# Attention of six batches in blocks of two head pairs, spread over the tiles of an MLP

## The chip, the cores and the metric

The kernel runs on one core of one Trainium2 chip. The metric is the time of one execution in microseconds (us), taken on the device. The core has TensorE (PE in the profile; its weight loads are listed apart as PEld), VectorE (DVE), ScalarE (ACT), GpSimd (POOL) and SyncE (SP), which here only issues DMA transfers.

## What is computed

The reference is a decayed causal attention followed by a mixture of four experts:

```python
# q, k, v: (8 batches, 8 heads, 576 positions, 64)
scores = scale * np.matmul(q, k.transpose(0, 1, 3, 2))
Dmat = np.where(rel >= 0, gamma ** rel, 0.0)        # gamma of the head, rel = i - j
attn = np.matmul(scores * Dmat, v)
x = attn.transpose(0, 2, 1, 3).reshape(8 * 576, 512)
p = domain_probs / domain_probs.sum(-1, keepdims=True)
for e in range(4):                                  # w1: 512 x 1024, w2: 1024 x 512
    out += p[:, e:e + 1] * (np.maximum(x @ w1[e], 0.0) @ w2[e])
```

There is no softmax, so the attention can be done in chunks of 128 positions: inside a chunk with scores and a triangular mask, and across chunks with a running state k^T v.

## The kernel before

**The MLP.** The 4608 rows of x are cut into nine tiles of 512. A batch has 576 rows, so batches and tiles do not line up: batch b ends 64(b+1) rows into tile b+1. Each tile has an up phase of 16 groups (`up_group`: eight matmuls of 512 columns into one PSUM tile `ph`, L358, then on DVE relu and the mixing weight in one instruction, L364) and a down phase. In tile 0 the down phase is plain (`down_plain`, L377). In tiles 1 to 8 it is two halves of seven products each (`Down.product`, L450, 16 matmuls of 256 columns per product, all seven into one PSUM tile `pd`), and DVE forms sums of h for them (`Down.sums`, L425 to L431). So a tile has 30 steps, called slots here: 16 up groups and 14 products. Weights w1 and w2 are loaded from POOL's DMA queue while tile 0 runs.

**Attention.** Batch 0 is done at the start, before tile 0, and batch 1 inside tile 0, both by `Unit`. Batches 2 to 7 are done by `Pair`, one batch in each of the tiles 1 to 6, one head pair at a time:

- `cast`: k by DVE (L241) and q by POOL (L245), each times its decay, and v by ACT (L249), from the single float32 buffers raw1 to bfloat16 buffers (two sets, `bfs`).
- `trans_dma`: two DMA transposes on SP's queue (L254), of k and of q, into one tile qkT.
- `load_pair`: six DMA loads on SP's queue (L76) of the next head pair into raw1.
- `scores`: eight matmuls with 64 contraction rows (64*128 in the profile), L274, then the mask on DVE (L276) into sT.
- `kv`: eight matmuls with 64 output columns of the array (128*64), L261, of 256, 192, 128 and 64 columns, which give the running state of all four chunks at once; ACT copies them to `sbd` (L266).
- `values`: three matmuls states x q^T of shape 128*128 (L284), then the next pair's scores and kv, then eight matmuls v x sT of shape 128*64 (L291), all values into one PSUM tile o; ACT copies o to the rows of x (`xt`, L298).

The last 64 positions of a batch, the remainder, are done by `Rem` for all heads at once: load (`load_rem`, five DMAs on SP), cast, two transposes, scores and values.

**PSUM.** `ph`, `pd`, o, s, `kvp` and the remainder's tiles all come from one pool of four buffers, called the ring here. A new tile has to wait until whoever reads its buffer's last tile is done.

**Order.** The schedule is written out by hand: each engine gets its instructions in program order. A dictionary `slots` holds, per slot of a tile, the functions to emit after that step:

```python
attention(slots, t + 1, (2, 7, 12, 18), (7, 11, 17, 22, 27))
```

The first tuple gives the slots of the four casts (each with its transposes and the next pair's loads), the second those of the five attention groups. The remainder of a batch is loaded at slot 21, cast at 26, and has its scores and values at slots 2 and 4 of the following tile.

**Memory.** The pool `early` holds the inputs of batch 0 and is closed before h is allocated. `later_tables` (L174) builds the mask and position tables on POOL, among the first weight loads.

Of the kernel before, what the change touches and what calls it, by code (L numbers as in the profile page):

```python
# [9 lines left out]
FP32 = mybir.dt.float32  # L10
# [13 lines left out]
def kernel(  # L24
# [16 lines left out]
    C = 128  # L41
# [49 lines left out]
    q1 = const.tile([128, 2, 2, 4, D], BF16, name="q1")  # L91
    raw2 = const.tile([128, 3, 2 * NC * D], FP32, name="raw2")
# [140 lines left out]
    class Pair:  # L233
        def __init__(self, b, p):
            self.b, self.p = b, p
            self.bf = bfs[p % 2]

        def cast(self, raw, n):
            p = self.p
            if n == "k":  # L240
                nc.vector.tensor_tensor(  # L241
                    self.bf["k"], raw["k"],
                    gk[:, :, 2 * p:2 * p + 2].unsqueeze(3).to_broadcast([128, NC, 2, D]), op=MULT)
            elif n == "q":
                nc.gpsimd.tensor_tensor(  # L245
                    self.bf["q"], raw["q"],
                    gq[:, :, 2 * p:2 * p + 2].unsqueeze(3).to_broadcast([128, NC, 2, D]), op=MULT)
            else:
                nc.scalar.activation(self.bf[n], raw[n], Copy)  # L249

        def trans_dma(self):
            self.qkT = atp.tile([128, 2, NC, C], BF16, tag="qkT", name="qkT")
            for i, n in ((1, "k"), (0, "q")):
                nc.sync.dma_start_transpose(  # L254
                    out=self.qkT[:, i, :, :], in_=self.bf[n][:, :, :, :].rearrange("p c h d -> p (c h d)"))

        def kv(self):
            kvp = ring_tile("kvp", [128, NC, D])
            for c in range(NC):
                for j in range(2):  # L260
                    nc.tensor.matmul(kvp[64 * j:64 * j + 64, c:NC, :], lhsT=self.bf["k"][:, c, j, :],  # L261
                                     rhs=self.bf["v"][:, c, j, :].unsqueeze(1).to_broadcast([128, NC - c, D]),
                                     start=(c == 0), stop=(c == NC - 1), skip_group_check=True)
            for j in range(2):
                r = slice(64 * j, 64 * j + 64)
                nc.scalar.activation(sbd[r, self.p, :, r], kvp[r, :, :], Copy)  # L266

        def scores(self):
            self.sT = atp.tile([128, 2, NC, C], BF16, tag="sT", name="sT")
            s = ring_tile("s", [128, 2, NC, C])  # L270
            for c in range(NC):
                for j in range(2):
                    r = slice(64 * j, 64 * j + 64)
                    nc.tensor.matmul(s[:, j, c, :], lhsT=self.qkT[r, 1, c, :], rhs=self.qkT[r, 0, c, :],  # L274
                                     start=True, stop=True)
            nc.vector.tensor_tensor(  # L276
                self.sT[:, :, :, :].rearrange("p j c t -> p (j c) t"), s[:, :, :, :].rearrange("p j c t -> p (j c) t"),
                tri[:, :].unsqueeze(1).to_broadcast([128, 2 * NC, C]), op=MULT)

        def values(self, following=None):  # L280
            b, p = self.b, self.p
            o = ring_tile("o", [128, SM])
            for c in range(1, NC):
                nc.tensor.matmul(o[:, c * C:(c + 1) * C], lhsT=sbd[:, p, c - 1, :], rhs=self.qkT[:, 0, c, :],  # L284
                                 start=(c == 1), stop=False, skip_group_check=True)
            if following is not None:
                following.scores()
                following.kv()
            for c in range(NC):
                for j in range(2):  # L290
                    nc.tensor.matmul(o[64 * j:64 * j + 64, c * C:(c + 1) * C], lhsT=self.bf["v"][:, c, j, :],  # L291
                                     rhs=self.sT[:, j, c, :], start=False, stop=(c == NC - 1), skip_group_check=True)
            n0 = b * S
            a = 0
            while a < SM:
                t = (n0 + a) // NT
                z = min(SM, (t + 1) * NT - n0)
                nc.scalar.activation(xt_of(t)[:, p, n0 + a - t * NT:n0 + z - t * NT], o[:, a:z], Copy)  # L298
                a = z

# [358 lines left out]
    mixing_weights()  # L659
    raw1u = {n: raw1[n][:, :, :, :].rearrange("p c j d -> p (c j d)") for n in "kqv"}  # L660
# [19 lines left out]
    later_tables()  # L680
# [9 lines left out]
    early.close()  # L690
    hp = ctx.enter_context(tc.tile_pool(name="hp", bufs=1))
    h = hp.tile([128, E * NFC, NT], BF16, name="h")


    def attention(slots, b, cast_at, head_at):
        add = lambda i, f: slots.setdefault(i, []).append(f)
        xs = [Pair(b, p) for p in range(NP)]
        add(head_at[0], xs[0].scores)
        add(head_at[0], xs[0].kv)
        for p in range(NP):  # L700
            add(head_at[p + 1], lambda p=p: xs[p].values(xs[p + 1] if p + 1 < NP else None))
# [134 lines left out]
```

## Time and profile before

| | before |
|---|---|
| median of 8 runs | 542.39 us (542.12 to 547.78) |
| the profiled execution | 542.32 us |
| its span, first to last instruction | 540.6 us |
| PE busy | 530.2 us, 98% |
| DVE busy | 366.6 us, 68% |
| ACT busy | 112.2 us, 21% |
| POOL busy | 91.3 us, 17% |
| DMA queue of SP (q1) | 43.50 MB, 35.7% of 16 engines |
| DMA queue of POOL (q0) | 19.27 MB, 16.2% |
| tiles 1 to 6, each, in the stretches of the trace | 57.8 to 57.9 us |
| tiles 7 and 8 | 52.6 and 52.1 us |

Busy time is when an engine executes; matmuls are pipelined, so their listed lengths overlap and PE's busy share says little about how well it is used. In a timeline, the differences between starts count. The bracket at the end of a timeline line is idle time of that engine just before, and what ended it. A line of waits gives who waited for whom, with total us, times and the longest. In the lines `128*128`, `64*128` and `128*64` are the rows and columns of the array that a matmul uses. The granted clock of TensorE is 1.0 in every slice.

### The profile page before, as it was taken

What the parts mean: (1) busy time and instruction counts of PE and PEld (TensorE: products, weight loads), DVE (VectorE), ACT (ScalarE), POOL (GpSimd) and SP (SyncE); (2) the same over time, 40 slices, a digit from 0 to 9 for tenths busy, and PEclk for the clock granted to TensorE, in tenths of its full rate; (3) what the DMA queues carried; (4) which work ended last, traced back from release to release, by engine and by line L of the source; (5) the groups of instructions that cost most, each with busy time, mean ns of one, the idle gap of its engine ahead of it and who ended that gap; (6) DMA issues with size and microseconds to landing.
All of it is one profiled execution on the core that took longest, in us unless ns stands there. A gap on an engine that the chain in (4) does not pass through costs nothing.

```text
span 540.6 us, 10292 instructions
## 1 busy us (share of the span) xinstructions
PE 530.2 (98%) x4279; PEld 341.1 (63%) x4319; DVE 366.6 (68%) x484; ACT 112.2 (21%) x255; POOL 91.3 (17%) x126
## 2 busy tenths in 40 slices
PE   8999999999999999999999999999999999999997
PEld 4544454568745884488547864687458844884486
DVE  5525669987488757876688648774886677557764
ACT  4723451122111320223022111131112200000010
POOL 5734002120211110211112111112111100010000
PEclk9999999999999999999999999999999999999999
DMA  9999947865266635665277517652564211110001
GB/s 237 206 213 249 228 124 185 145 158 119 84 118 134 142 100 101 140 114 142 70 154 128 147 55 137 149 140 89 102 135 117 77 47 39 41 41 21 0 27 54
DMA packets 145119, 63.56 MB, mean 118 GB/s; under 512 B 124240, under 2 KB 135888, under 8 KB 145072
## 3 DMA queue, kind: packets, MB, share of 16 engines
q1 hardware_dynamic: 134752, 43.50, 35.7%
q0 software_dynamic: 10176, 19.27, 16.2%
q8 instruction: 34, 0.56, 0.4%
q14 instruction: 13, 0.11, 0.1%
q10 hardware_dynamic: 144, 0.13, 0.1%
HBM read 53.56 MB, written 9.51 MB: 117 GB/s over the span
## 4 chain that ended last, share of the span: by engine, by line
PE 92%; DVE 4%; ACT 1%; DMA 1%; issue 1%; SPq 0%; DVEq 0%; ACTq 0%
PE ph L358 44%; PE pd L450 37%; PE po L377 4%; DVE h L364 2%; PE kvp L261 1%; PE s L274 1%; PE o L291 1%; ACT qkT L518 1%; PE pt L516 1%; DMA raw_0q<-in_q_dram 1%; PE o L284 1%; PE s L539 0%; DMA qkT<-bf_q 0%; DVE sT L541 0%; PE kvp L558 0%
## 5 line engine op out<-in xcount | busy, mean ns | idle before, releaser
L358 PE MATMUL ph<-xt,w 128*128 128x512 bf16 x1118 | 252.5, 379 | 3.1 <-DVE h L364 1.2
L358 PEld LDWEIGHTS <-w 128*128 128x128 bf16 x1152 | 110.8, 98 | 129.4 <-issue 1.7
L364 DVE SCALAR_TENSOR_TENSOR h<-ph,pB 128x1024 bf16<-128x1024 f32 x128 | 156.0, 1222 | 51.8 <-PE ph L358 51.5
L450 PEld LDWEIGHTS <-h 128*128 128x128 bf16 x1024 | 99.2, 98 | 14.1
L450 PEld LDWEIGHTS <-s 128*128 128x128 bf16 x768 | 74.6, 98 | 9.1
L450 PE MATMUL pd<-wx,h 128*128 128x256 bf16 x512 | 61.3, 273 | 0.0
L450 PE MATMUL pd<-wx,s 128*128 128x256 bf16 x512 | 61.2, 273 | 0.0
L222 POOL DMA_DIRECT2D pB<-pd x28 | 15.8, 566 | 169.1 <-DVE h L364 137.5
L266 ACT ACTIVATE sbd<-kvp 64x256 bf16<-64x256 f32 x48 | 18.1, 378 | 106.4 <-PE kvp L261 106.1
L485 POOL TENSOR_TENSOR ob<-v,p 128x256 f32<-128x256 f32 x15 | 10.9, 724 | 148.3 <-DVE v L482 92.4
L276 DVE TENSOR_TENSOR sT<-s,tri 128x1024 bf16<-128x1024 f32 x24 | 29.2, 1217 | 2.1 <-PE s L274 2.1
L450 PE MATMUL pd<-t4w,h 128*128 128x256 bf16 x256 | 30.6, 273 | 0.0
L450 PE MATMUL pd<-t3w,h 128*128 128x256 bf16 x256 | 30.6, 273 | 0.0
L450 PE MATMUL pd<-t2w,s 128*128 128x256 bf16 x256 | 30.6, 273 | 0.0
L245 POOL TENSOR_TENSOR bf_q<-raw_q,gq 128x512 bf16<-128x512 f32 x24 | 26.0, 1083 | 26.3 <-DMA raw_q<-in_q_dram 20.6
L467 DVE TENSOR_TENSOR u<-pd,p 128x256 f32<-128x256 f32 x16 | 6.8, 425 | 33.0 <-PE pd L450 33.0
L377 PE MATMUL po<-wx,h 128*128 128x512 bf16 x124 | 28.4, 379 | 0.3 <-issue 0.2
L458 ACT ACTIVATE p<-pd 128x256 f32<-128x256 f32 x16 | 6.1, 383 | 92.8 <-PE pd L450 88.7
L431 DVE TENSOR_TENSOR s<-h,s 128x1024 bf16<-128x1024 bf16 x32 | 24.2, 796 | 0.0
L469 DVE TENSOR_TENSOR oa<-pd,u 128x256 f32<-128x256 f32 x16 | 6.8, 425 | 23.7 <-PE pd L450 23.7
L249 ACT ACTIVATE bf_v<-raw_v 128x512 bf16<-128x512 f32 x24 | 15.1, 629 | 32.4 <-DMA raw_v<-in_v_dram 32.4
L429 DVE TENSOR_TENSOR h<-h 128x1024 bf16<-128x1024 bf16 x32 | 21.4, 709 | 0.0
(147 smaller groups left out, 390.8 us busy)
## 6 DMA issues: line engine op xcount, KB each, us to landing
pB<-pd POOLq DMA_DIRECT2D x28, 256.0 KB, 3.9
raw_k<-in_k_dram SPq DMA_DIRECT2D x48, 128.0 KB, 2.8
raw_q<-in_q_dram SPq DMA_DIRECT2D x48, 128.0 KB, 3.1
raw_v<-in_v_dram SPq DMA_DIRECT2D x48, 128.0 KB, 3.8
wx<-in_moe_w_dram POOLq DMA_DIRECT2D x4, 1024.0 KB, 15.2
out_dram<-oa SPq DMA_DIRECT2D x16, 256.0 KB, 2.1
out_dram<-ob SPq DMA_DIRECT2D x15, 256.0 KB, 2.1
w<-in_moe_w_dram POOLq DMA_DIRECT2D x3, 1024.0 KB, 14.9
```

Of the source, the lines that this page charges most:

```text
L222: eng.dma_start(out=pB[t, e], in_=pd[e:e + 1, t * NT:(t + 1) * NT].to_broadcast([128, NT]))
L245: nc.gpsimd.tensor_tensor(self.bf["q"], raw["q"], gq[:, :, 2 * p:2 * p + 2].unsqueeze(3).to_broadcast([128, NC, 2, D]), op=MULT)
L249: nc.scalar.activation(self.bf[n], raw[n], Copy)
L266: nc.scalar.activation(sbd[r, self.p, :, r], kvp[r, :, :], Copy)
L276: nc.vector.tensor_tensor(self.sT[:, :, :, :].rearrange("p j c t -> p (j c) t"), s[:, :, :, :].rearrange("p j c t -> p (j c) t"), tri[:, : ...
L358: nc.tensor.matmul(ph[:, f, :], lhsT=w1_sb[e][:, dc, fc * 128:(fc + 1) * 128], rhs=x[:, dc, :], start=(dc == 0), stop=(dc == NDC - 1))
L364: nc.vector.scalar_tensor_tensor(h[:, fk:fk + 2, :], ph, 0.0, pB[t, e][:, :].unsqueeze(1).to_broadcast([128, 2, NT]), op0=MAX, op1=MULT)
L377: nc.tensor.matmul(po[:, g, :], lhsT=h[:, e * NFC + fc, ns * 128:(ns + 1) * 128], rhs=wx[e // 2][:, (e % 2) * NFC + fc, :, :].rearrange("p ...
L429: nc.vector.tensor_tensor(h[:, l, self.b], h[:, l, self.a], h[:, l, self.b], op=SUB)
L431: nc.vector.tensor_tensor(self.alloc("s4")[:, l], h[:, r, self.a], self.s2[:, l], op=SUB)
L450: mm = nc.tensor.matmul(dst, lhsT=src[:, kk, tok], rhs=rhs(c), start=(start and c == 0), stop=(c == KH - 1), skip_group_check=True)
L485: nc.gpsimd.tensor_tensor(self.ob[:, HF:Dm], self.v, self.p5, op=ADD)
```

## The change

The class `Pair` becomes `Duo`, two head pairs, and `attention` goes. A function `block(new, old)` emits the kv of the two new pairs, the values (v x sT first, then the states) of the two pairs in front of them, and the scores of the new ones. The PSUM tile `kvp` holds two pairs, and so does o; ACT copies them with instructions twice as long and half as many. Scores and masks stay one tile and one DVE instruction a pair. k^T and q^T get tiles of their own (two and four buffers), v gets four buffers.

Slots are now numbered through all tiles (30 a tile, from tile 1 on), and blocks, casts and loads are placed by four hand-written rules: for batches 2, 3, 4 and for 5 to 7. Batch 2 to 4 blocks stand at slots 9, 18, 27, 36, 44 and 64, later ones at slots 13 of a tile and 4 of the following one. The first block has no values, and a last one at slot 163 has values only. Casts are at 1, 5, 10, 14, 19, 23, 27, 31, 36, 40, 45, 51 and then at slots 5, 9, 15 and 21 of a tile. Remainders are moved as well.

To make room, q1 and raw2 (used by batch 1 only) leave the constant pool for a pool `fpool` that is closed after tile 0, and the new tiles take their place. For that `early` is closed, and h is allocated, ahead of the first weight loads, and `later_tables` is moved from behind the second weight load issued there to ahead of the first one (w2 of expert 0).

```diff
-    class Pair:
...
+    class Duo:
...
+        def cast(self, p):
+            for n, eng, g in (("k", nc.vector, gk), ("q", nc.gpsimd, gq)):
+                eng.tensor_tensor(bfs[p % 2][n], raw1[n],
+                                  g[:, :, 2 * p:2 * p + 2].unsqueeze(3).to_broadcast([128, NC, 2, D]), op=MULT)
+            nc.scalar.activation(bv[p], raw1["v"], Copy)
+            self.kT[p] = dpl.tile([128, NC, C], BF16, tag="kT", name="kT", bufs=2)
+            self.qT[p] = dpl.tile([128, NC, C], BF16, tag="qT", name="qT", bufs=4)
+            for t, n in ((self.kT[p], "k"), (self.qT[p], "q")):
+                nc.sync.dma_start_transpose(out=t, in_=bfs[p % 2][n][:, :, :, :].rearrange("p c h d -> p (c h d)"))
...
         def kv(self):
-            kvp = ring_tile("kvp", [128, NC, D])
+            kvp = ring_tile("kvp", [128, 2, NC, D])
+            for i, p in self.pairs():
+                for c in range(NC):
+                    for j in range(2):
+                        nc.tensor.matmul(kvp[64 * j:64 * j + 64, i, c:NC, :], lhsT=bfs[p % 2]["k"][:, c, j, :],
...
             for j in range(2):
                 r = slice(64 * j, 64 * j + 64)
-                nc.scalar.activation(sbd[r, self.p, :, r], kvp[r, :, :], Copy)
+                nc.scalar.activation(sbd[r, self.ps, :, r], kvp[r], Copy)
...
+        def values(self):
+            o = ring_tile("o", [128, 2, SM])
+            for i, p in self.pairs():
...
+                        nc.tensor.matmul(o[64 * j:64 * j + 64, i, c * C:(c + 1) * C], lhsT=bv[p][:, c, j, :],
+                                         rhs=self.sT[p][:, j, c, :], start=(c == 0), stop=False, skip_group_check=True)
+            for i, p in self.pairs():
+                for c in range(1, NC):
+                    nc.tensor.matmul(o[:, i, c * C:(c + 1) * C], lhsT=sbd[:, p, c - 1, :], rhs=self.qT[p][:, c, :],
+                                     start=False, stop=(c == NC - 1), skip_group_check=True)
...
+    def block(new, old):
+        if new is not None:
+            new.kv()
+        if old is not None:
+            old.values()
+        if new is not None:
+            new.scores()
...
     mixing_weights()
+    later_tables()
+    early.close()
+    hp = ctx.enter_context(tc.tile_pool(name="hp", bufs=1))
+    h = hp.tile([128, E * NFC, NT], BF16, name="h")
+    first = ctx.enter_context(ExitStack())
+    fpool = first.enter_context(tc.tile_pool(name="fpool", bufs=1))
...
     load_w2(0)
     load_w1(1)
-    later_tables()
     load_w2(1)
...
+        if b == 2:
+            cast_at, block_at, rem_at = (1, 5, 10, 14), (9, 18), (8, 13, 21, 24)
+        elif b == 3:
+            cast_at, block_at, rem_at = (19, 23, 27, 31), (27, 36), (25, 32, 38, 40)
+        elif b == 4:
+            cast_at, block_at, rem_at = (36, 40, 45, 51), (44, 64), (47, 57, 67, 69)
+        else:
+            cast_at, block_at, rem_at = (g + 5, g + 9, g + 15, g + 21), (g + 13, g + 34), (g + 17, g + 27, g + 37, g + 39)
...
+            add(block_at[d], lambda new=duos[d], old=old: block(new, old))
+            old = duos[d]
...
+    add(NS * 5 + 13, lambda old=old: block(None, old))
...
-        if t + 1 < B:
-            attention(slots, t + 1, (2, 7, 12, 18), (7, 11, 17, 22, 27))
```

## The prediction

> **What bounds the kernel now.** I read the page first, then the time by stage, then TensorE's timeline inside one tile, then the waits, then SP's queue.
>
> ```profile
> PE 530.2 (98%) x4279; PEld 341.1 (63%) x4319; DVE 366.6 (68%) x484; ACT 112.2 (21%) x255; POOL 91.3 (17%) x126
> ...
> PE 92%; DVE 4%; ACT 1%; DMA 1%; issue 1%; SPq 0%; DVEq 0%; ACTq 0%
> ```
>
> TensorE is busy almost throughout and is 92% of the chain that ended last. A change to attention pays only as far as it shortens TensorE's own sequence. Stretches of a tile with attention and of the last tile, which has none (start:end, length, then busy us by engine):
>
> ```profile
> 316.60:374.40 57.80, 57.40 (x470) 38.53 (x473) 41.79 (x50) 11.15 (x28) 9.62 (x11) 1.00 0.53 120
> 484.90:537.00 52.10, 51.87 (x349) 34.23 (x350) 33.32 (x42) 2.30 (x6) 2.17 (x3) 1.00 0.06 21
> ```
>
> One batch with its remainder costs 57.8 - 52.1 = 5.7 us of TensorE's line, at the full clock (1.00). Now two groups of `Pair.values` (start, length, instruction; the bracket is idle time and who ended it):
>
> ```profile
> 280.73 0.33 PE L284 MATMUL o<-qkT,sbd 128*128 128x128 bf16 x3
> 280.99 0.40 PE L274 MATMUL s<-qkT 64*128 64x128 bf16 x8
> 281.32 0.47 PE L261 MATMUL kvp<-bf_v,bf_k 128*64 128x256 bf16 x8
> 281.62 0.39 PE L291 MATMUL o<-sT,bf_v 128*64 128x128 bf16 x8
> 282.21 7.07 PE L358 MATMUL ph<-xt,w 128*128 128x512 bf16 x31 [0.20 <-DVE h L364]
> ...
> 292.60 0.33 PE L284 MATMUL o<-qkT,sbd 128*128 128x128 bf16 x3
> 292.87 0.40 PE L274 MATMUL s<-qkT 64*128 64x128 bf16 x8
> 293.19 0.47 PE L261 MATMUL kvp<-bf_v,bf_k 128*64 128x256 bf16 x8
> 293.49 0.39 PE L291 MATMUL o<-sT,bf_v 128*64 128x128 bf16 x8
> 293.82 1.92 PE L450 MATMUL pd<-wx,h 128*128 128x256 bf16 x16
> ```
>
> Read starts, since lengths overlap in the pipeline. Sixteen `ph` matmuls of 512 columns take 3.45 us in the chain, 0.42 ns a column, so 128 columns are 0.055 us. Three states matmuls: 0.165 us, yet the scores start 0.27 us later: 0.10 lost. Eight scores run as four pairs on two halves of the array: 0.22, next start after 0.32: 0.10 lost. `kvp`: four pairs of 256, 192, 128 and 64 columns, 0.27; next start after 0.30. `kvp` and the values share the shape 128*64, and nothing but 0.03 is lost between them. Values 0.22, next start after 0.33: 0.10 lost. So each change of the shape in the row (128*128, 64*128, 128*64) costs 0.10 us. The group is 1.22 us, of which 0.30 is three such changes.
>
> ```profile
> PE ph L358 <- DVE h L364: 1.2, 5, 0.4
> PE s L274 <- DMA qkT<-bf_q: 0.2, 1, 0.2
> ACT bf_v L249 <- DMA raw_v<-in_v_dram: 32.4, 15, 4.2
> ```
>
> These waits are the rest (total, times, longest). In the timeline the group at 280.7 would have ended at 281.95 and `ph` starts at 282.21: o, s and `kvp` take three of the four ring buffers, so the next `ph` needs the buffer of the last one, which DVE is still emptying. This costs 0.26 in four tiles and 0.50 in the first (108.25 to 108.75); one scores group waited 0.27 for its transpose. Sum 1.8 us. The third line says that ACT often waits for v: loads come just in time.
>
> **Shape changes on TensorE.** Before, per batch: the head group (full, 64*128, 128*64, full) three changes, three middle groups three each, the last group two: 14, or 84 in six batches. After, a block is kv, values, states, scores: 128*64, 128*128, 64*128 and back, four changes for two pairs. Eleven full blocks, a first one without values (three) and a last one without new pairs (two): 49. 35 fewer at 0.10 = -3.5 us. The matmuls themselves are the same. The step from 64*128 back to 128*128 is in no group above; between 0.03 (no change of shape) and 0.20 (double) it moves the sum by -0.8 to +1.2 over 12 blocks; I take 0.10, the value of every neighbour. The Trainium skill ("TensorE: Matmul & The Clock Gate", Single matmul latency) gives a lone matmul a warm constant of 398 cycles at 2.4 GHz, 166 ns; if each change exposed all of it, 35 would be worth 5.8 us, but the rows show 0.10.
>
> A block is then 2x0.30 + 2x0.23 + 6x0.055 + 2x0.23 + 4x0.10 = 2.25 us; with its two missing parts the first is 1.36, the last 0.99.
>
> **The old stalls.** The `ph` stalls came from groups of three ring tiles right after a `ph` in the up phase. A block takes four tiles (`kvp`, o, s, s). Its second s needs the buffer of the `ph` just before it, but begins 1.9 us into the block, and DVE has emptied that `ph` after 1.27. The 0.27 of the scores goes too: scores now come last in a block, 1.5 us behind its start. -1.8 us. What is late next: the `ph` after a block needs `kvp`'s buffer. ACT starts on `kvp` 0.23 after its last matmul (293.47 to 293.70), 0.91 into the block, and now reads 512 columns twice. No row has 512 on 64 partitions:
>
> ```profile
> L298 ACT ACTIVATE xt<-o 128x448 bf16<-128x448 f32 x4 | 2.2, 538 | 0.0
> ...
> L266 ACT ACTIVATE sbd<-kvp 64x256 bf16<-64x256 f32 x48 | 18.1, 378 | 106.4 <-PE kvp L261 106.1
> ```
>
> Between them a column costs 0.83 ns, so 512 take 0.59 us; twice the 378 (0.76) is the other end. ACT is done 0.91 + 2x0.59 + 0.05 = 2.15 us into the block, 0.10 before TensorE wants the buffer: no cost, but thin cover. ACT's evictions of o, 1.25 us behind this, are needed a whole `ph` later.
>
> Two blocks, at slots 18 and 27, stand in tile 1's product phase, where `pd` holds a ring buffer. The fourth tile of the block can then only have `kvp`'s buffer: the second s wants it at 1.9 and gets it at 2.15. 2 x 0.25 = +0.5 us. DVE does two masks (2x1.22) before the sums queued behind them there; the products that read s4 and h follow 3.5 and 5.3 us later, which just covers them.
>
> A rule speaks against the change: the Trainium skill ("TensorEngine Tiling (Array Packing)", PSUM Bottleneck) warns that packing speeds TensorE but not PSUM evacuation. Taken strictly, with all of a block's PSUM evicted before the next `ph` (ACT until 3.4 us), eleven blocks would each lose 1.1 us, an estimate of +12 us; but the ring makes `ph` wait for `kvp` alone.
>
> **Transfers and SP's queue.** Each pair still issues two transposes and six loads from SP, and raw1 is still single: the next load waits for the casts. What moves is their pace in tiles 1 and 2. Casts were 5 or 6 slots apart; now they are 4 or 5 from slot 1 to 45.
>
> ```profile
> 92.39 1.19 SPq L254 DMA_TRANSPOSE qkT<-bf_k  x1
> 93.67 1.22 SPq L254 DMA_TRANSPOSE qkT<-bf_q  x1
> 94.95 1.12 SPq L76 DMA_DIRECT2D raw_k<-in_k_dram  x2
> 96.11 1.59 SPq L76 DMA_DIRECT2D raw_q<-in_q_dram  x2
> 97.80 1.00 SPq L76 DMA_DIRECT2D raw_v<-in_v_dram  x2
> ```
>
> SP works 6.4 us per pair. The chain that repeats is k's cast 0.7, transposes 2.5, two k issues 1.1, landing 2.8 (median of the DMA table): 7.1 us. From slot 1 to 31 there are seven such periods, 49.7 us, and SP also carries two remainder loads (2x3.2), two remainder transposes (2.4) and outputs (2.0): 10.8, of which 7x0.7 fits under the landings. Need 55.6. On TensorE the same slots take 30x1.735 + 1.36 + 2x2.25 + 0.35 = 58.3. It fits by under 3 us. Where a load is late DVE waits at its k cast, and the `ph` evictions and product sums queue behind it; following the rows, casts 14 and 23 find raw_k landing about as DVE gets there, and the cover (ring and products) is 1 to 1.5 us. I charge +0.4, from 0 to +3. From slot 51 on casts are 14, 4, 6 and 6 apart, nearly as loose as before; DVE carries 2 masks per block in the up phase, about 27.5 us of work in 32.4.
>
> The remainder's loads, casts and transposes only change slot; POOL's q casts (1.08 each, 17% busy) and pB loads keep their order; new tiles q1, raw2, kT, qT and v share memory whose last readers are done by tile 0's end. All at nothing, since all are off TensorE.
>
> **Start.** later_tables (POOL, 16.91 to 20.09, 3.1 us) goes ahead of the first w2 load, issued at 15.29 and landed 10.3 later, at 25.6; `po` needs it at 27.6. POOL would issue it at 18.4. The queue was busy with w1's second half until 20.1 anyway, and its first packets came 2.75 after the issue, so at 21.2: 1.1 us late, landing 26.7, still 0.9 ahead. Nothing; if the whole 3.1 arrived, +1.1.
>
> **Sum.** The profiled execution took 542.32 us (span 540.6), 0.07 under the median 542.39, so I work against it: 542.3 - 3.5 - 1.8 + 0.5 + 0.4 = 537.9 us.
>
> **Rivals.** (a) Eviction takes the place of the shape changes: if ACT needs 0.76 per half of `kvp`, it is done at 2.48, each of nine full up-phase blocks loses 0.24 and the two others 0.33 more: +2.8, 540.7, no difference to measure (a measurement here tells about 0.5%, 2.7 us). For it: the cover is only 0.10. Against: the column slope of the rows. (b) Slower: SP's issue cannot hold the four-slot pace. Single loads took 1.2 to 1.7 us to issue instead of 0.55 (the 2.12 pair at 117.46). If each of the 11 casts up to slot 44 ran 1.1 us over my count, 12 us of need against 3 + 2 of slack gives +7: 545 us; from 1.1 us per cast it decides against the change. For it: ACT's 15 waits for v. Against: before, one pair in four was hit, once per pair. Half of that overrun gives (a)'s time. (c) The shape changes do not go away, for instance because the states group waits behind the values' writes in the same o: then only the stalls are gained, 541.4.
>
> **How the numbers follow.** Forecast 537.9, own range 536.4 (return step free, no charge for loads) to 539.4: 0.66. (a) and a mild (b): 0.16; (c): 0.07; (b) in full or a late w2: 0.11. The range 536.3 to 541.6 takes in the first three. Faster by over 0.5% (below 539.7): 0.68; within: 0.21; slower: 0.11.
>
> **What would show it.** TensorE's timeline of a block should read `kvp` x16, o x16, o x6, s x16, then `ph`, 2.25 us from start to start, without an idle bracket; tiles 3 to 6 last 56.9 instead of 57.8. Wrong steps would show as `ph` or s waiting for ACT sbd (a), DVE waiting for raw_k and TensorE for DVE or qT in tile 1 (b), `po` waiting for wx near 27.

## The result, and the profile after

The changed kernel takes 546.7 us (median of 11 runs, 544.5 to 552.2), beside 542.43 us for the kernel before on the same chip: ratio 1.0085, interval 1.0065 to 1.0104. It is slower by 4 us where the forecast was faster by 4.5. The profiled execution took 546.48 us, its span 544.8.

The page after, in the lines that answer to those of before (busy time, and the chain that ended last by engine):

```profile
PE 529.6 (97%) x4279; PEld 340.6 (63%) x4319; DVE 371.0 (68%) x484; ACT 105.5 (19%) x207; POOL 91.1 (17%) x126
...
PE 76%; SPq 9%; DMA 8%; DVE 3%; issue 2%; POOL 1%; ACT 0%; DVEq 0%; POOLq 0%
```

TensorE had 92% of the chain and has 76%; SP's queue and the DMA engines together went from about 1% to 17%. Its busy time is 529.6 us against 530.2, so its own sequence did not become longer. Something that was hidden is now on the path.

Where it is, the stretches of tiles 1 to 5 show (start:end, length, then busy us of PE, PEld, DVE, ACT and POOL; at the end the granted clock, the DMA share and GB/s):

```profile
85.60:150.70 65.10, 61.09 (x514) 40.69 (x516) 49.22 (x61) 13.79 (x27) 13.31 (x14) 0.97 0.77 159
150.70:209.60 58.90, 56.95 (x471) 38.33 (x474) 44.88 (x52) 11.29 (x22) 11.86 (x13) 1.00 0.73 159
209.60:266.50 56.90, 56.69 (x470) 38.28 (x472) 42.29 (x50) 10.12 (x20) 9.55 (x11) 1.00 0.58 122
266.50:323.40 56.90, 56.69 (x470) 38.28 (x472) 42.67 (x50) 10.06 (x20) 9.29 (x11) 1.00 0.52 122
323.40:381.30 57.90, 56.91 (x470) 38.30 (x472) 43.30 (x50) 10.14 (x20) 9.32 (x11) 1.00 0.48 107
```

Tiles 3 and 4 are the 56.9 us of the forecast; tile 5 misses it by one wait for qT of 0.8, and tile 6, at 55.7, is shorter than it because it has only one full block and the last one. Tile 1 lasts 65.1. Cut in the same way at the first `ph` matmul of each tile (us, one profiled execution each; tiles 7 and 8 up to the start of the last matmul; the last two rows are experiments told below):

| | tile 0 | 1 | 2 | 3 | 4 | 5 | 6 | 7 and 8 |
|---|---|---|---|---|---|---|---|---|
| before | 64.8 | 58.3 | 57.8 | 57.8 | 57.8 | 57.8 | 57.8 | 104.2 |
| after | 65.2 | 65.1 | 58.7 | 56.9 | 56.9 | 57.8 | 55.7 | 104.1 |
| after, without pair loads of batches 2 to 4 | 66.0 | 59.8 | 56.9 | 56.9 | 56.9 | 58.2 | 55.7 | 104.1 |
| blocks inside the batch's own tile, old start | 64.8 | 57.5 | 57.1 | 57.4 | 57.1 | 58.1 | 57.1 | 104.4 |

The loss is tile 1 with +6.8, tile 2 with +0.9 and tile 0 with +0.4; tiles 3 to 6 give back 3.9. Sum +4.1, against a span longer by 4.2.

First, what the change was to do. TensorE's timeline through one block in tile 3 (start, length, instruction):

```profile
218.22 0.75 PE L255 MATMUL kvp<-v,bf_k 128*64 128x256 bf16 x16
218.80 0.62 PE L280 MATMUL o<-sT,bf_v 128*64 128x128 bf16 x16
219.34 0.51 PE L284 MATMUL o<-qT,sbd 128*128 128x128 bf16 x6
219.79 0.62 PE L269 MATMUL s<-qT,kT 64*128 64x128 bf16 x16
220.34 2.33 PE L359 MATMUL ph<-xt,w 128*128 128x512 bf16 x9
```

The order is the one forecast, and no line has a bracket of idle time. Read the starts: `kvp` takes 0.58 (0.54 by its columns, and no change of the shape behind it), the values 0.54 (0.44 and one change), the states 0.45 (0.33 and one), the scores 0.55 (0.44 and one). So a change costs 0.10 to 0.12, and the step back from 64*128 to 128*128 costs as much as the others. With the one ahead of `kvp` the block is 2.22 us, where 2.25 was forecast. ACT's eviction of `kvp`, whose cover was thin, came out at the interpolated 0.59 us (busy us and mean ns, then the idle time before it):

```profile
L260 ACT ACTIVATE sbd<-kvp 64x512 bf16<-64x512 f32 x24 | 14.2, 591 | 73.1 <-PE kvp L255 72.0 <-ACT xt L350 0.9
```

Second, the new waits (who waited for whom: total us, times, longest):

```profile
POOL bf_q L239 <- DMA raw_q<-in_q_dram: 70.3, 12, 7.4
ACT v L241 <- DMA raw_v<-in_v_dram: 52.3, 12, 8.5
DVE bf_k L239 <- DMA raw_k<-in_k_dram: 14.8, 8, 2.7
...
PE sr L338 <- DMA qTr<-bfr_q: 1.7, 1, 1.7
PE pd L451 <- ACT p L459: 1.3, 1, 1.3
PE ph L359 <- DVE h L365: 1.2, 2, 0.8
PE s L269 <- DMA qT<-bf_q: 0.8, 1, 0.8
```

DVE waits for raw_k at eight of its casts; before, it waited for raw_k at none in tiles 1 to 6. The waits of TensorE below it have several names and one root. One of them in the timelines of ACT and of TensorE (start, length, instruction; in the bracket the idle time before it and its releaser):

```profile
121.01 0.63 ACT L241 ACTIVATE v<-raw_v 128x512 bf16<-128x512 f32 x1 [7.12 <-DMA raw_v<-in_v_dram]
121.66 0.38 ACT L459 ACTIVATE p<-pd 128x256 f32<-128x256 f32 x1
```

```profile
120.44 0.39 PE L451 MATMUL pd<-t4w,h 128*128 128x256 bf16 x2 [0.56 <-DVE h L365]
122.09 2.28 PE L451 MATMUL pd<-wx,h 128*128 128x256 bf16 x14 [1.26 <-ACT p L459]
```

"TensorE waits for ACT p" is really the v load. In ACT's program order the eviction of product 1 stands behind a v cast that waited for raw_v until 121.0, and it starts when this cast is done. Product 2 needs that eviction. What follows costs more than the wait (windows of one us; the figure before the last two is the granted clock):

```profile
122.00:123.00 1.00, 0.91 (x9) 0.81 (x9) 1.00 (x3) 0.04 (x1) 0.00 (x0) 1.00 0.62 129
123.00:124.00 1.00, 1.00 (x8) 0.71 (x6) 0.39 (x1) 0.00 (x0) 0.00 (x0) 0.52 1.09 198
...
126.00:127.00 1.00, 1.00 (x24) 0.90 (x18) 0.00 (x0) 0.93 (x2) 0.00 (x0) 0.78 0.58 113
```

TensorE runs at half the clock for 3.4 us, 1.7 us lost. Stalls in tiles 1 and 2, read from the gaps between matmul starts beyond their columns: 0.57, 0.96, 0.73, 1.43, 0.27, 0.79 and 1.85 us, 6.6 in all, and the clock: 8.3. Of these the 0.27 is not a late load: it is the wait of the second s for `kvp`'s buffer that the forecast had charged.

The DMA table of the stretch from 86 to 187 us, tiles 1 and 2 in the main, says what is late (KB each, median us from issue to landing). Before:

```profile
raw_k<-in_k_dram SPq DMA_DIRECT2D x16, 128.0 KB, 2.8
```

After:

```profile
raw_k<-in_k_dram SPq DMA_DIRECT2D x20, 128.0 KB, 3.8
...
pB<-pd POOLq DMA_DIRECT2D x8, 256.0 KB, 4.1
...
kT<-bf_k SPq DMA_TRANSPOSE x10, 3.2
```

The landing that I put at 2.8 us is 3.8, and the transposes before it land in 3.2 instead of 2.4. SP and GpSimd at one cast (their timelines):

```profile
92.36 1.19 SPq L245 DMA_TRANSPOSE kT<-bf_k  x1
93.64 1.22 SPq L245 DMA_TRANSPOSE qT<-bf_q  x1
94.91 1.12 SPq L76 DMA_DIRECT2D raw_k<-in_k_dram  x2
96.07 1.05 SPq L76 DMA_DIRECT2D raw_q<-in_q_dram  x2
97.23 2.39 SPq L76 DMA_DIRECT2D raw_v<-in_v_dram  x2
100.92 1.20 SPq L245 DMA_TRANSPOSE kT<-bf_k  x1
```

```profile
94.64 0.60 POOL L220 DMA_DIRECT2D pB<-pd  x1 [3.12 <-DVE h L365]
```

A pB load of 256 KB is issued 0.3 us ahead of the pair's raw_k, and at the next three casts again 0.1 to 2.1 us ahead (103.46 and 103.56, 112.06 and 114.16, 120.97 and 122.90): the buffer of pB and the next cast both wait for DVE. Six pair loads are 768 KB, so it adds a third to what has to land. SP is not always free either: six of the first ten transposes of k start 0.3 to 1.3 us after their cast is done (4.7 us in all), because SP still issues transfers of a remainder or of the output; before, all eight in this stretch start 0.06 us behind their cast.

### The profile page after: what moved, and what is told of

Same layout as the page of the kernel before. It is cut to its first block, busy times and chain, and to the rows that moved or that the text cites. A ratio compares the mean times of both kernels' runs of the same rounds, so it can differ in the third digit from the quotient of the medians.

```text
span 544.8 us, 10272 instructions
## 1 busy us (share of the span) xinstructions
PE 529.6 (97%) x4279; PEld 340.6 (63%) x4319; DVE 371.0 (68%) x484; ACT 105.5 (19%) x207; POOL 91.1 (17%) x126
## 4 chain that ended last, share of the span: by engine, by line
PE 76%; SPq 9%; DMA 8%; DVE 3%; issue 2%; POOL 1%; ACT 0%; DVEq 0%; POOLq 0%
PE ph L359 36%; PE pd L451 31%; PE po L378 4%; SPq L76 4%; DMA raw_q<-in_q_dram 3%; SPq L245 2%; DMA wx<-in_moe_w_dram 2%; SPq L117 1%; DMA raw_v<-in_v_dram 1%; DMA raw_3v<-in_v_dram 1%; PE kvp L255 1%; PE s L269 1%; DMA qT<-bf_q 1%; PE o L280 1%; PE o L284 1%
## 5 line engine op out<-in xcount | busy, mean ns | idle before, releaser
L451 PEld LDWEIGHTS <-h 128*128 128x128 bf16 x1024 | 100.4, 98 | 15.9 <-issue 1.6
L486 POOL TENSOR_TENSOR ob<-v,p 128x256 f32<-128x256 f32 x15 | 10.9, 725 | 133.6 <-DVE v L483 105.5
L239 DVE TENSOR_TENSOR bf_k<-raw_k,gk 128x512 bf16<-128x512 f32 x24 | 18.3, 764 | 14.8 <-DMA raw_k<-in_k_dram 14.8
L260 ACT ACTIVATE sbd<-kvp 64x512 bf16<-64x512 f32 x24 | 14.2, 591 | 73.1 <-PE kvp L255 72.0
L426 DVE TENSOR_TENSOR s<-h 128x1024 bf16<-128x1024 bf16 x32 | 28.3, 923 | 0.0
L459 ACT ACTIVATE p<-pd 128x256 f32<-128x256 f32 x16 | 6.1, 381 | 108.6 <-PE pd L451 104.4
L428 DVE TENSOR_TENSOR s<-s,h 128x1024 bf16<-128x1024 bf16 x32 | 24.0, 788 | 0.0
L432 DVE TENSOR_TENSOR s<-h,s 128x1024 bf16<-128x1024 bf16 x32 | 21.4, 706 | 0.0
## 6 DMA issues: line engine op xcount, KB each, us to landing
w<-in_moe_w_dram POOLq DMA_DIRECT2D x3, 1024.0 KB, 14.8
```

The costliest lines, as they stand in the source:

```text
L239: eng.tensor_tensor(bfs[p % 2][n], raw1[n], g[:, :, 2 * p:2 * p + 2].unsqueeze(3).to_broadcast([128, NC, 2, D]), op=MULT)
L260: nc.scalar.activation(sbd[r, self.ps, :, r], kvp[r], Copy)
L426: nc.vector.tensor_tensor(self.alloc("s1")[:, l], h[:, l, self.b], h[:, r, self.b], op=ADD)
L428: nc.vector.tensor_tensor(self.alloc("s2")[:, l], self.s1[:, l], h[:, l, self.a], op=SUB)
L432: nc.vector.tensor_tensor(self.alloc("s4")[:, l], h[:, r, self.a], self.s2[:, l], op=SUB)
L451: mm = nc.tensor.matmul(dst, lhsT=src[:, kk, tok], rhs=rhs(c), start=(start and c == 0), stop=(c == KH - 1), skip_group_check=True)
```

## The experiments

Theories. **Landing**: the dense casts ask for more than the DMA engines deliver beside the pB loads, and DVE, ACT and the transposes then wait in their order. **Issue**: SP cannot issue it all (the forecast's slower rival). **Order on ACT**: it is the v casts that hold up evictions. **Blocks**: blocks that reach over tiles cost the time by themselves. All ratios are to the kernel before on the same chip; each edit is to the changed kernel, and `...` marks what is left out of it.

### Pace, and blocks inside the tile

Casts spread to five or six slots in tiles 1 and 2:

```diff
-            cast_at, block_at, rem_at = (1, 5, 10, 14), (9, 18), (8, 13, 21, 24)
+            cast_at, block_at, rem_at = (1, 6, 11, 16), (11, 21), (8, 18, 24, 26)
...
+            if b == 2 and d == 1:
+                add(28, lambda old=old: block(None, old))
+                old = None
```

> The blocks stay, but the casts of batches 2 to 4 are spread evenly, 5 to 6 slots apart (1, 6, 11, 16, 21, 26, 31, 36, 41, 46, 52, 58), and the blocks follow them (11, 21, 28, 31, 41, 52, 64; the one at 28 has values only). Pace theory (the loss in tiles 1 and 2 is the load chain, which needs 9.6 us a pair while four slots give 7): DVE no longer waits for raw_k there, the clock stays at 1.0, tiles 1 and 2 lose some 7 us of the waits, 538.5 to 540 us. Block theory (the loss is that blocks stand in product phases, where they hold the ring and ACT): three blocks stand there now instead of two, so 546 us or more.

542.1 us, 0.9996 (0.9979 to 1.0013). 4.6 us of the loss go with the pace; tile 1 is 60.0. That is less than the 538.5 to 540 of the pace theory: DVE still waits for raw_k, five times and 6.9 us in all (eight times and 14.8 us before this edit). Blocks and remainders move with the casts here, so the pace isn't changed alone.

Every batch in its own tile, with the casts at the slots that they had before the change; a block of values alone ends each batch:

```diff
+g = NS * (b - 2)
+cast_at, block_at, rem_at = (g + 2, g + 7, g + 12, g + 18), (g + 11, g + 22), (g + 21, g + 26, g + 32, g + 34)
...
+add(g + 27, lambda old=old: block(None, old))
```

> Blocks of two pairs, but each batch within its own tile as before the change: casts at slots 2, 7, 12, 18, blocks at 11 (new pairs only), 22 and 27 (values only), remainders as before. 14 changes of shape a batch become 9, and the casts keep the old pace. Pace theory: 542.3 - 3.0 (30 changes) - 1.8 (old stalls) + 0.5 (start) + about 0.3 (ring at slot 22) = 538.3 us. Block theory: two blocks a batch stand in product phases, so slower than 542.4.

539.9 us, 0.9948 (0.9933 to 0.9963): faster than before, by 2.5 us where its sum had 4.0. So blocks of two pairs do pay, and it is their reach over tiles, or the density of casts that goes with it, that costs.

### Loads left out

```diff
             if p + 1 < NP:
-                add(at, lambda b=b, p=p: load_pair(raw1, b, p + 1))
+                if b > 4:
+                    add(at, lambda b=b, p=p: load_pair(raw1, b, p + 1))
-            elif b + 1 < B:
+            elif 3 < b < B - 1:
                 add(at, lambda b=b: load_pair(raw1, b + 1, 0))
```

> Leaves out part of the work: the pairs of batches 2 to 4 aren't loaded again, and are cast from what the first load of batch 2 left (casts, transposes, blocks and all slots stay). If the landing of these loads is what the dense slots run into, the stalls of tiles 1 and 2 go (0.57, 0.96, 0.73, 1.43, 0.27, 0.79, 1.85 us and about 1.7 for the clock dip: 8.3 in all), the late w2 (0.5) and the stall of tile 5 (0.9) stay: 546.5 - 8.3 = 538.2 us. If blocks that reach over tiles cost the time by themselves, or transposes and casts do, it stays above 543.

540.2 us, 0.9963 (0.9947 to 0.9979). The blocks, casts, transposes and slots are those of the changed kernel, and 6.5 us go: tile 2 is 56.9 and tile 1 59.8, of which 0.8 is one wait for qT. The theory of the blocks falls; the pair loads make the loss. Whether by their data or by their issues this run can't tell, since both go. The profiled execution had a late start (tile 0 at 66.0) and took 542.2, so it is not the best of its runs.

### Who issues, and in which order

Remainder loads of batches 2 to 4 from GpSimd:

```diff
-add(rem_at[0], lambda b=b: load_rem(b))
+add(rem_at[0], lambda b=b: load_rem(b, nc.gpsimd if b < 5 else nc.sync))
```

> The changed kernel with the remainder loads of batches 2 to 4 (five DMAs each, 3.2 to 4.0 us of SP) issued by POOL instead. Pace theory: SP is freed of 3.2 us or more at slots 8, 25 and 47, the casts behind come earlier by that much, and 2 to 4 us of the loss go: 542.5 to 544.5 us. If landing times alone set the pace (the DMA engines are over 100% busy around 116 to 120 us), the bytes are the same and it stays at 546 us.

549.7 us, 1.0130 (1.0114 to 1.0145). v loads from ScalarE:

```diff
-                eng.dma_start(out=t[n][:, :, j, :],
+                (nc.scalar if n == "v" else eng).dma_start(out=t[n][:, :, j, :],
```

> The v loads of pairs are issued by ScalarE behind its v cast, so SP has two issues of 0.5 to 2.3 us fewer per pair; the bytes and their times are nearly the same. If the time that SP takes to issue is the matter, the period of casts falls by 1.5 to 2 us and most stalls go: 540 to 542. If the landing of the data is, no gain: 545 to 548.

548.9 us, 1.0120 (1.0098 to 1.0142). In both SP has less to issue, and neither gains. With v from ScalarE raw_k still lands in 3.9 us, in the same stretch of the trace. This speaks against the theory of the issue, but not alone: GpSimd and ScalarE, which issue instead, have casts in the same chain. The runs below that keep every issue and move fewer bytes weigh more. The Trainium skill ("DMA: Bandwidth & Descriptors", Issuing engines are not separate DMA queues) says that transfers started by several engines run on the same 16 DMA engines and interleave, so that another issuer saves only issue time; these runs agree that it gains nothing here.

v casts and v loads two slots later, behind k and q:

```diff
+            for i, which in ((0, "kq"), (2, "v")):
+                if which == "v":
+                    add(at + i, lambda d=duos[p // 2], p=p: d.cast_v(p))
+                if p + 1 < NP:
+                    add(at + i, lambda b=b, p=p, which=which: load_pair(raw1, b, p + 1, which=which))
...
```

> The v cast and v load of each pair come two slots behind its k and q; nothing else moves. If ScalarE's order is the matter (evictions of products and of the values behind a v cast that waits for its load), the two waits on ScalarE (1.43 and 0.79) and the clock dip (1.7) go: about 542.5 to 543.5. If the landing is, ScalarE's waits go but VectorE's k casts come no sooner, and the time stays within 2 us of 546.5. SP then issues k before the last v load, so k may also come sooner by 1 us per pair.

546.2 us, 1.0077 (1.0047 to 1.0106). No product waits for ACT any more, and the time stays, because the same lateness shows at the next place:

```profile
PE s L271 <- DMA qT<-bf_q: 4.6, 3, 2.1
```

So order on ACT is one of the ways in which the loss came out; taking it away wins nothing.

Loads ahead of the transposes on SP:

```diff
+        def trans(self, p):
             for t, n in ((self.kT[p], "k"), (self.qT[p], "q")):
...
                 add(at, lambda b=b: load_pair(raw1, b + 1, 0))
+            add(at, lambda d=duos[p // 2], p=p: d.trans(p))
```

> The next pair's six loads are issued ahead of the two transposes instead of behind them. If the chain k cast, transposes, k issues, landing sets the pace, its period falls by the transposes' 2.5 us and the k waits of tile 1 mostly go: 541 to 543. But the transposes start 3 to 4 us later, and scores whose block stands four slots (7 us) behind the cast may wait for qT: up to +1 for each of three blocks, 545 to 548. If the DMA engines' bytes set the pace, no gain from the order of issue at all: 546 or more.

Its four executions took 563.1 to 572.3 us, median 571.1; the ratio, 1.0443 (1.0368 to 1.0517), is that of the two shortest, 563.1 and 570.0. My highest figure was 548. Scores wait for the transposes in seven blocks, also in tiles whose pace is easy, and the transposes now take 4.5 us (median) to land instead of 2.6:

```profile
PE s L271 <- DMA qT<-bf_q: 21.5, 7, 4.4
...
kT<-bf_k SPq DMA_TRANSPOSE x24, 4.5
```

After six of these seven waits (2.5 to 4.4 us) TensorE's clock is at half for 3.4 us. raw_k does land in 2.7 us in the stretch from 86 to 187, and it doesn't help. Of these two orders of issue the changed kernel's is the better one.

### Rows, bytes and what runs beside

Another order of the tokens in the load, meant to give rows of 1 KB:

```diff
-in_=src[b, 2 * p + j, 0:SM, :].rearrange("(c p) d -> p c d", p=C)
+in_=src[b, 2 * p + j, 0:SM, :].rearrange("(p c) d -> p c d", p=C)
```

> The pair loads take tokens in another order (partition p gets tokens 4p to 4p+3 of a head), so that the same bytes move in rows of 1 KB instead of 256 bytes; the tokens are permuted in the result. Issues, casts and slots stay. If small rows make the landing long, raw_k lands in 2 to 2.5 us instead of 3.7, the last raw_v is issued in 0.5 us, and the stalls of tiles 1 and 2 go: 538 to 540. If bytes or the chain on SP set the pace, 545 or more.

548.5 us, 1.0113 (1.0085 to 1.0141). This run says nothing on rows, since the page's packets are those of the changed kernel, all the same. The tile that they go to still takes 256 bytes (64 values) at a time, which is the likely reason:

```profile
DMA packets 145118, 63.56 MB, mean 116 GB/s; under 512 B 124240, under 2 KB 135888, under 8 KB 145072
```

Half of each pair load:

```diff
-                eng.dma_start(out=t[n][:, :, j, :],
-                              in_=src[b, 2 * p + j, 0:SM, :].rearrange("(c p) d -> p c d", p=C))
+                lo = 0 if (b, p) == (2, 0) else NC // 2
+                eng.dma_start(out=t[n][:, lo:NC, j, :],
+                              in_=src[b, 2 * p + j, lo * C:SM, :].rearrange("(c p) d -> p c d", p=C))
```

> Leaves out half of every pair load (two of the four chunks; the rest stays as it was after the first load): the same issues, with half the rows and half the bytes. Where rows or bytes set the landing, the stalls go: 538 to 540; where the number of issues or a fixed latency does, 545 or more. Beside the run with long rows it tells rows from bytes: both fast means rows, only this one means bytes.

541.4 us, 0.9986 (0.9968 to 1.0004), with 48 issues of each kind as before: 5.3 us less with the number of issues kept. So it is the data and not the number of issues; rows and bytes were halved together, and stay untold apart.

Without the pB loads of tiles 2 and 3:

```diff
-        if i == NFC // 2 - 1 and t + 1 < n_nt:
+        if i == NFC // 2 - 1 and t in (1, 2):
+            pB[t + 1, e] = pB[t, e]
+        elif i == NFC // 2 - 1 and t + 1 < n_nt:
             load_p(t + 1, e, nc.gpsimd)
```

> Leaves out the pB loads for tiles 2 and 3 (these tiles are weighted with the pB of tile 1); 2 MB fewer bytes, on GpSimd's queue, while the dense casts run. If the transfers that run beside the pair loads stretch their landing, raw_k lands again near 2.8 us and most of the stalls of tiles 1 and 2 go: 541 to 543. If SP's own queue and its pair loads set it, within 1.5 us of 546.5.

541.1 us, 0.9978 (0.9960 to 0.9997). Taking 2 MB of another engine's loads away does nearly as much as taking all pair loads of batches 2 to 4 away. In the same stretch as above, with all pair loads in place:

```profile
raw_k<-in_k_dram SPq DMA_DIRECT2D x22, 128.0 KB, 2.6
```

It could still be the place of the pB issues on GpSimd, ahead of the q casts. Two runs bear on this. The same bytes, issued by ScalarE:

```diff
-            load_p(t + 1, e, nc.gpsimd)
+            load_p(t + 1, e, nc.scalar)
```

> The pB loads are issued by ScalarE instead of GpSimd; their bytes stay. If GpSimd's order was the matter, q casts come earlier and most of the 5.5 us is won: 541 to 543. If the bytes were, 545 to 548, since the pB loads land beside the pair loads as before (ScalarE also pays 0.6 us per issue and may hold evictions).

548.7 us, 1.0118 (1.0103 to 1.0133). And half the bytes in the same place:

```diff
-    pd = dpool.tile([E, N], FP32, name="pd")
+    pd = dpool.tile([E, N], BF16, name="pd")
...
-        pB[t, e] = ppool.tile([128, NT], FP32, tag="pB", name="pB")
+        pB[t, e] = ppool.tile([128, NT], BF16, tag="pB", name="pB")
```

> The mixing weights are written to DRAM and read back as bf16: each pB load moves 128 KB instead of 256, with the same issues in the same places on GpSimd. If the bytes beside the pair loads stretch their landing, half of the 5.5 us that leaving out the pB loads of tiles 2 and 3 brought comes here, or more: 541.5 to 544. If it was the order on GpSimd (q casts queued behind pB issues that wait for their buffer), the time stays: 546 or more.

544.4 us, 1.0039 (1.0013 to 1.0065), 2.3 us under the changed kernel. With GpSimd's order kept, half of pB's bytes are worth 2.3 of the 5.6 us, and DVE's instruction that reads pB takes 1.22 us as before, so the gain is not a faster DVE. The run with pB from ScalarE proves less than it seems: ScalarE now waits four times, 18.2 us in all, for DVE to free pB's buffer, ahead of its v casts. So bytes count for certain; that order on GpSimd has no part at all is not shown.

Taken together: in tiles 1 and 2 the pair loads and the pB loads come later than the casts want them, and fewer bytes of either help. Two things stay open. By which mechanism a pB load stretches a pair load inside the DMA engines, no run here shows. And the landing of raw_k alone doesn't put the runs in order: in the same stretch its median is 3.3 us both with pB from ScalarE (548.7) and with half loads (541.4). The period from one k cast to the next comes nearer. On average over ten it is 9.6 us in the changed kernel, 9.4 with bf16, 9.1 with half loads, 9.0 without the pB loads and 8.9 without pair loads, but 9.4 as well with pB from ScalarE, where waits for qT (4.8 us in all) and a halved clock are added.

### The start

The late tables back behind the second weight load:

```diff
-    later_tables()
...
     load_w1(1)
+    later_tables()
     load_w2(1)
```

> The changed kernel with later_tables back behind the second weight load. Start theory: the first w2 lands in time again, po starts 0.4 to 0.5 us earlier (27.6 to 27.8 in the trace), and the whole gains 0.5 us, about 546.2. Rival (the weights land late because the other loads around them differ): po still starts at 28.1.

548.9 us, 1.0123 (1.0092 to 1.0154); inconclusive, since in the profile an input came late at the start and the first w2 load was issued at 16.75 instead of 15.29, so `po` still waited, and tiles 1 and 2 varied by more than the term. The whole old order of the loads at the start was then put into kernels without the large stalls. First with blocks inside the tile:

```diff
     mixing_weights()
+    load_w2(0); load_w1(1)
     later_tables()
+    load_w2(1); load_rem(0, nc.gpsimd); load_w1(2); load_w2(2)
     early.close()
...
-    load_w2(0); load_w1(1); load_w2(1); load_rem(0, nc.gpsimd); load_w1(2); load_w2(2)
```

> Blocks inside each batch's own tile (as in the run with 539.9), and the loads at the start in the old order, with the late tables behind the first w2 and w1 loads. If the tables' place costs the start 0.4 to 0.5, then 539.4 to 539.5 and no wait of po for wx; if the wait at the start comes from something else, 539.9 again, with the wait still there.

539.4 us, 0.9944 (0.9927 to 0.9961), beside 539.9. And in the kernel without the pB loads of tiles 2 and 3, with the same edit:

> As the run without the pB loads of tiles 2 and 3 (left out here too), with the loads at the start in the old order, ahead of the late tables. po waited for w2 between 0.4 and 2.3 us in all runs with the tables first, by profile; if the tables' place is the cause, that wait is gone here and the median falls from 541.1 by 0.5 to 1.5 us. If not, 541 again with the wait.

539.8 us, 0.9956 (0.9942 to 0.9971), beside 541.1. Tile 0 is 64.8 in each profile with the old order, and from 64.8 (one run, with bf16) to 67.0 with the tables first. First the wait in the kernel without these pB loads and with the tables first, then the window of two us in the changed kernel in which its DMA engines run half empty (0.52 in the last column but one; before, 1.23):

```profile
PE po L380 <- DMA wx<-in_moe_w_dram: 1.5, 1, 1.5
```

```profile
18.00:20.00 2.00, 1.95 (x44) 1.15 (x42) 1.93 (x4) 0.92 (x3) 2.00 (x4) 1.00 0.52 78
```

So the new order at the start costs 0.5 to 1.3 us by the medians. The intervals of either pair of runs overlap; what supports the term is the wait of `po` for w2, which is gone in the profiles of both runs with the old order.

### Put together

Even pace, old start, pB as bf16, and some casts and the remainder scores of batch 3 moved against late transposes:

```diff
-cast_at, block_at = (g + 5, g + 9, g + 15, g + 21), (g + 13, g + 34)   # batches 5 to 7; the rest as above
+cast_at, block_at = (g + 3, g + 8, g + 15, g + 21), (g + 13, g + 34)
```

> Computes everything. The even pace of casts (542.1 us), with the old order of the loads at the start (-0.9), pB as bf16 (-0.5 to -1.5), remainder scores of batch 3 two slots later (-1), and from batch 5 on the first two casts one or two slots earlier, so that the transpose of the second is not late for its block (-1): 537.5 to 539. If the landing stays tight, 540 to 541, no better than the blocks inside the tile with 539.4.

538.7 us, 0.9942 (0.9925 to 0.9959), but its first sentence does not hold: the cast at g + 3 stands ahead of the block at g + 4, which then takes k^T v of its first pair from the k of the following batch, so this is not the time of the whole computation. With that mended:

```diff
+cast_at, block_at = (g + 4, g + 9, g + 15, g + 21), (g + 14, g + 34)   # batches 5 to 7
```

> Computes everything: even pace of casts, loads at the start in the old order, pB as bf16, remainder scores of batch 3 two slots later, and from batch 5 on the first two casts at g+4 and g+9 with their block at g+14 (the cast at g+4 stands behind the block of the batch before, in the same slot). Without late transposes it should give 538 to 539; if the landing stays tight, 540 or more.

539.7 us, 0.9939 (0.9916 to 0.9961), above the 538 to 539 that were hoped for.

The same with pd and pB in 32 bits:

> As the one before, with pB in 32 bits as in both kernels. If the even pace and the start are enough, 538 to 539 as well; if the bytes of pB still decide at this pace, 0.5 to 1.5 us more than with bf16.

541.1 us, 0.9961 (0.9942 to 0.9981). At the even pace the bytes of pB are still worth 1.4 us by the medians, though the intervals overlap. Four versions that compute everything beat both kernels: blocks inside the tile with the old start (539.4) and without it (539.9), the even pace with bf16 weights (539.7), and the same without (541.1).

## Why the prediction was wrong

**Right: the shape changes.** 0.10 to 0.12 each, the return step too; no wait of the second s in the up phase, and 0.27 in the one block of the product phase that ran at the full clock, where 0.25 was charged; `kvp`'s eviction 0.59 us; tiles 3 and 4 at 56.9. With tile 1 of the run without pair loads less its one wait (59.8 - 0.8 = 59.0), 56.9 for tiles 2 to 5 (tile 5 reaches it in the run with half loads) and 55.7, the structure by itself is 58.3 + 5 x 57.8 - 59.0 - 4 x 56.9 - 55.7 = 5.0 us shorter than before; the forecast's terms for it were 3.5 + 1.8 - 0.5 = 4.8. Rivals (a) and (c) did not happen.

**Wrong: the term for the load pace.** It was put at +0.4, at most +3. It is about +8.8: 6.1 in tile 1 (65.1 less 59.0), 1.8 in tile 2 and 0.9 in tile 5. The step that failed is "landing 2.8 (median of the DMA table)": a median over tiles whose DMA engines have room was used in a stretch in which the change itself packs the pairs' loads closer. There it is 3.8, and the transposes land in 3.2 us instead of 2.4. From the first k cast in tile 1 on, ten periods last 9.6 us on average, and 8.9 in the run without pair loads. The slack of under 3 us in 58 was seen and taken for cover; seven periods with 1 us more each use it up twice over. SP's other work was not the step: 5.9 us were charged for it over these seven periods, and the late starts of the transposes come to 3.5.

The median also hid a row of the old profile. Before the change, the first pair load of tile 1 is issued 1.2 us behind a pB load (transfers issued from 93.7 to 96.2 us, KB each, us to landing):

```profile
pB<-pd POOLq DMA_DIRECT2D x1, 256.0 KB, 4.1
raw_k<-in_k_dram SPq DMA_DIRECT2D x2, 128.0 KB, 4.2
```

The next one is issued after the next pB load has landed (from 105.5 to 107 us):

```profile
raw_k<-in_k_dram SPq DMA_DIRECT2D x2, 128.0 KB, 2.7
```

Tiles 2 and 3 begin in the same way, with 4.1 and 4.0 us beside a pB load. So a landing of 4 us beside a pB load could be read before the change, and the change puts more casts beside one.

**Wrong: "all at nothing, since all are off TensorE"**, said of the pB loads, among others. They kept their place, but their bytes ran beside transfers that had become tight, and were worth 5.6 us.

**Half right: the slower rival.** (b) gave 545 and the sign, and the trace looks like it, with two raw_v issues that take 2.4 us together. But its mechanism was issue on SP; taking issues off SP did not help in two runs, and halving the data with all issues kept won 5.3 us. That 545 is near the result is in part luck. I gave it 0.11, together with a late w2, because I asked only whether SP has the time and not whether the DMA engines do.

**Missing: what a late load does next.** The sum took lateness beyond the cover as lost time and no more. In the trace it was passed on (v cast, then product 1's eviction, then product 2), and the halved clock that came 0.9 us after this wait cost another 1.7 us.

**Start.** "Nothing; if the whole 3.1 arrived, +1.1": w2 landed at 28.0 instead of 26.7. Tile 0 is 0.4 us longer in the profile, and the order of the loads is worth 0.5 to 1.3 us in the two pairs of runs, within their noise. The argument was that the queue was busy until 20.1 anyway; but before, w2's load ran beside the end of w1's (DMA share 1.23 from 18 to 20 us), and with the tables first the DMA engines ran half empty there (0.52).

## What to carry to other kernels

When a schedule packs the same transfers into less time, do not carry a landing time over from the old profile (here 2.8 us became 3.8), and look at which of its landings were beside another load: add up all bytes that land in that stretch, those of other queues too, and hold them against what the stretch carried before (131 GB/s in tiles 1 and 2 before, 161 after). A slack of 5% in a single-buffered load chain was no slack here. When waits with many names appear together, look for the one transfer behind them, and test by leaving out data, not by moving the wait: the five edits here that changed who issues, or in which order, gained nothing to speak of, the four that took bytes away gained 2.3 to 6.5 us, and spreading the casts gained 4.6.

## What the runs showed of the hardware

- Loads from one queue went with later landings on another. Eight pB loads of 256 KB fewer in 100 us, and 128 KB loads of raw_k land in 2.6 us instead of 3.8; before the change they took 4.2 us just behind a pB load and 2.7 clear of one.
- Starting the transfers from another engine did not help: 548.7 us with pB from ScalarE, 548.9 with v from ScalarE, 549.7 with the remainders from GpSimd, beside 546.7.
- TensorE's clock was halved for 3.4 us after waits of 0.56 and 1.26 us within 2.2 us, while a single wait of 1.7 in tile 2 left it at 1.00. The length of a wait doesn't decide it in the other profiles either: with pB from ScalarE it was halved for 3.4 us after a single wait of 1.96, and it stayed full through one of 2.77 (tables behind the weights) and one of 2.85 (pB as bf16). The Trainium skill ("TensorE: Matmul & The Clock Gate", Why this matters for your kernels) says to avoid idle gaps of over about 3 us; here shorter ones were enough, and the measurement decides. What decides between these cases, no run here shows.
- DMA transposes that are issued behind six loads land in 4.5 us in the median, against 2.6 ahead of them, and scores four slots behind the cast did not cover that (seven waits, 21.5 us).
- The changed kernel, whose loads are just late, has no settled time: 544.5 to 552.2 us in eleven runs, beside 539.1 to 540.2 in four with blocks inside the tile.
